# More filler matmuls and wider pick matmuls in an attention-decode and gMLP kernel

## Chip, cores, metric

One core of one Trainium2 chip. The metric is the device time of one execution in microseconds, lower is better. Before: 651.57 us, median of 6 runs (651.5 to 651.92). The span in the profile is about 1.4 us shorter than the measured time (650.2 against 651.6 us), because it runs from the first to the last recorded instruction.

## The reference

Branch A is attention for one query token with 32 heads over a cache of 16384 keys and values. Branch B is a small gated MLP on the same token. A sigmoid gate mixes them.

```python
q = (x @ wq) -> 32 heads of 128
scores = einsum('bhqd,bhkd->bhqk', q, k_cache) * 128 ** -0.5    # k_cache: 32 x 16384 x 128 bf16
p = softmax(scores); o = einsum('bhqk,bhkd->bhqd', p, v_cache)  # v_cache: the same size
a = o.reshape(1, 1, 4096) @ wo                                  # wo: 4096 x 512
b = gmlp(x)                                                     # a few MB of weights
return g * a + (1 - g) * b                                      # output: 1 x 1 x 512
```

K and V alone are 2 x 32 x 16384 x 128 x 2 bytes = 268 MB, and each byte is used once. With wq, wo and the MLP weights it is 279.6 MB.

## The kernel before

Heads are processed in 16 pairs. K and V of a pair are 8.4 MB each. The loads rotate through three buffers: K0, K1, V0, K2, V1, K3, ..., V14, V15 and then wo. A load waits until the buffer's last user has signalled. All the large loads are issued from one queue (SP).

For each pair VectorE (DVE) multiplies K by the query, TensorE (PE) sums parts of the products, DVE reduces, ScalarE (ACT) takes the exponential, and PE multiplies the weights with V. Four accumulators at array columns 0, 32, 64 and 96 collect the value sums. ACT copies them to SBUF, and four "pick" matmuls add the right rows into two columns of `o_ps` (the trace shows each of these fp32 matmuls as two, eight in all).

```python
    def warm(e, n):                 # n fillers of 128 columns, rhs all zeros
        for j in range(n):
            args = (m_ps[0], ident[:, :], zero[:, :])
            # ... the first loads weights, the others reuse them

    def fill(e, m, n=1):            # n fillers of m columns, at array column 96
        for _ in range(n):
            matmul_again(nc, e, m_ps[0][96:96 + m, :], ident[:, 0:m], zero[:, :], start=True,
                         stop=True, skip_group_check=True)

    def values(e, p, pa, va):
        # ... 8 groups: 8 value matmuls at columns 32 * (j % 4), one fill(e, 8)
        o2 = o_ps[:, bass.ds(value(e, p, NP - 1) * 2, 2)]
        fill(e, 8, 2)
        take(e, drn_s)                                  # ACT's copy of the accumulators
        for r in range(4):
            ins = e.matmul(o2, lhsT=d_sb[:, r * Dh:(r + 1) * Dh],
                           rhs=pick[:, r * 2:(r + 1) * 2], start=False, stop=False,
                           skip_group_check=True)
        ins.then_inc(pe.sem, 1)                         # frees the V buffer
```

Each filler streams 512 columns of zeros past m columns of the array (m is 128, 8 or 1; 379 ns each at the median, and two in a row start 0.215 us apart). The fillers write to a bank that nobody reads; their only use seems to be to keep PE busy, so that its clock stays up. The tail after the last pair normalizes o, transposes and gathers it with PE and DVE, and multiplies it by the 32 row blocks of wo. Sixteen blocks are done in four "wide" rounds, the other 16 in pairs of one-column matmuls at array columns 0 and 32. Those last rows wait for their part of wo.

```python
    def pe_wide(e):
        warm(e, 3)
        with e.Fori(0, WIDE // WG) as t:
            # ... 4 matmuls of one column, at columns 0, 32, 64, 96
            registers_first(nc, n, lambda: take(e, wo_s))
            ins.then_inc(pe.sem, 1)
            fill(e, 1)
            # ...
    # ACT copies d_ps to d_sb; then rows 16..31 of wo, each as two matmuls:
    for j, (a, b) in enumerate(zip(WO_CUTS[:-1], WO_CUTS[1:])):      # (0, 16, 24, 29, 31, 32)
        for k in range(max(a, WIDE), b):
            y_ok = add(o2[:, k:k + 1], wo[:, k * D:(k + 1) * D],
                       [(ld_o[j], 16)] if k == a else (), k == H - 1)
        if b == 24:
            add(ones_f[:, 0:1], d_sb[:, :], [w_ok])
```

The softmax here doesn't subtract the row's maximum and nothing guards it: scores larger than these inputs give would overflow.

Of the kernel before, what the change touches and what calls it, by code (L numbers as in the profile page):

```python
# [6 lines left out]
ALU = mybir.AluOpType  # L7
AX = mybir.AxisListType

FP32 = mybir.dt.float32  # L10
BF16 = mybir.dt.bfloat16

P = 128
Dh = 128
H = 32
NP = H // 2
# [16 lines left out]
NG = KP // 4  # L33
TG = 8
WG = 4
NT = NG // TG
ZB = F // 4
K_CUTS = (0, 128, 256)
# [45 lines left out]
def take(eng, sem, n=1):  # L84

    eng.wait_ge(sem, n).then_inc(sem, -n)  # L86
# [90 lines left out]
def gated_mix_kernel(nc, A_x, A_k_cache, A_v_cache, A_wq, A_wo, B_x, B_w_in, B_w_sp, B_b_sp,  # L177
                     B_w_out, gate_w, out):
    def sb(name, shape, dt):
        return nc.alloc_sbuf_tensor(name, shape, dt)  # L180
# [4 lines left out]
    p_t = sb("p_t", [P, 2 * NG * 8], BF16)  # L185
    s_sb = sb("s_sb", [P, KP], FP32)
    d_sb = sb("d_sb", [P, 512], FP32)
    zero = sb("zero", [P, 512], BF16)
# [6 lines left out]
    ident = sb("ident", [P, P], BF16)  # L195
    eps_t = sb("eps_t", [P, 1], FP32)
    sel = sb("sel", [H, 4 * (P + 1)], BF16)
    pick = sb("pick", [P, 4 * 2], FP32)
    wbf = sb("wbf", [P, 2], FP32)
    g_sb = sb("g_sb", [P, 1], FP32)  # L200
    gm_sb = sb("gm_sb", [P, 1], FP32)
# [9 lines left out]
    L_sb = sb("L_sb", [P, H], FP32)  # L211
# [3 lines left out]
    o2 = sb("o2", [P, H], BF16)  # L215
# [40 lines left out]
    pool, sp, pe, dve, act = (Queue(nc, e, n) for e, n in (  # L256
        (nc.gpsimd, "pool"), (nc.sync, "sp"), (nc.tensor, "pe"), (nc.vector, "dve"),
        (nc.scalar, "act")))
# [7 lines left out]
    def value(e, reg, top):  # L266
        return nc.snap(bass.RegisterHandles([reg]), min_val=0, max_val=top)
# [4 lines left out]
    ident_ok = pool.chain(lambda e: e.affine_select(  # L272
        out=ident[:, :], in_=ident[:, :], compare_op=ALU.not_equal, fill=1.0, base=0,
        pattern=[[-1, P]], channel_multiplier=1))
    for t in [sel, L_sb, p_t, zero]:
        p_zero = pool.op(lambda e, t=t: e.memset(t[:, :], 0.0), mark=True)
    sel_ok = (pool.sem, ident_ok[1] + 1)
    pool.raw(lambda e: e.nop().then_inc(exp_s, 1))


# [15 lines left out]
    for c in range(DC):  # L296
        x_ok = pe.op(lambda e, c=c: e.matmul(
            m_ps[1][:, c * P:(c + 1) * P], lhsT=x_row[0:1, c::DC], rhs=ones_row[0:1, :],
            start=True, stop=True), wait=[(ld_x, 16)] if c == 0 else (),
            mark=(c == DC - 1))  # L300
# [6 lines left out]
        out=sel[:, :].rearrange("h (i x) -> h i x", x=P + 1)[:, :, 0:P:4],  # L307
        in_=ident[0:H, 0:H].unsqueeze(1).broadcast_to([H, 4, H])), wait=[sel_ok],
        mark=True)
    dve.op(lambda e: e.tensor_reduce(  # L310
        out=pick[:, :].rearrange("p (r s) -> p s r", r=4),
        in_=ident[:, :].rearrange("p (g x) -> p x g", x=32)[:, 0:8, :]
        .rearrange("p (s r) g -> p s r g", r=4), axis=AX.X, op=ALU.add), wait=[ident_ok], mark=True)
    dve.op(lambda e: e.tensor_tensor(out=xg_row[:, :], in0=x_row[:, :], in1=gw_row[:, :],
                                     op=ALU.mult), wait=[(ld_g, 48)], mark=True)
    dve.op(lambda e: e.tensor_copy(out=xgw[:, 1:3], in_=wb_row[:, :]), mark=True)
    xgw_ok = dve.chain(lambda e: e.tensor_reduce(out=xgw[:, 0:1], in_=xg_row[:, :], axis=AX.X,  # L317
                                                 op=ALU.add))
# [3 lines left out]
                                    stop=True), wait=[xgw_ok], mark=True)  # L322
    act.op(lambda e: e.activation(out=g_sb[:, :], in_=g_ps[:, 0:1], func=ACT.Sigmoid),
           wait=[g_ok], mark=True)
# [54 lines left out]
    for h in range(2):  # L379
        zh = ps_all[:, 6 * h * 512:(6 * h + 2) * 512].rearrange("p (b x) -> p b x", b=2)[:, :, 0:ZB]  # L380
        dve.op(lambda e, h=h, zh=zh: e.tensor_tensor(  # L381
            out=zm[:, 2 * h * ZB:2 * (h + 1) * ZB].rearrange("p (b m k) -> p b m k", b=2, k=FhC),
# [5 lines left out]
        out=z[:, :].rearrange("p (e k) -> p e k", e=2),  # L388
        in_=zm.rearrange("p (e m k) -> p e k m", e=2, k=FhC), axis=AX.X, op=ALU.add))
    dve.chain(lambda e: e.scalar_tensor_tensor(  # L390
        out=zt[:, :], in0=z[:, :], scalar=0.044715, in1=z[:, :], op0=ALU.mult, op1=ALU.mult))
    zt_ok = dve.chain(lambda e: e.scalar_tensor_tensor(
        out=zt[:, :], in0=zt[:, :], scalar=1.0, in1=z[:, :], op0=ALU.add, op1=ALU.mult))
# [3 lines left out]
                  mark=True)  # L397
    dve.op(lambda e: e.tensor_tensor(out=z[:, :], in0=z[:, :], in1=zt[:, :], op=ALU.mult),
           wait=[sg_ok], mark=True)
    dve.chain(lambda e: e.tensor_reduce(out=stats[:, 0:1], in_=z[:, FhC:FC], axis=AX.X, op=ALU.add))  # L400
    dve.op(lambda e: e.tensor_tensor(out=sq[:, :], in0=z[:, FhC:FC], in1=z[:, FhC:FC],
                                     op=ALU.mult), mark=True)
    st_ok = dve.chain(lambda e: e.tensor_reduce(out=stats[:, 1:2], in_=sq[:, :], axis=AX.X,
                                                op=ALU.add))
    tot_ok = pe.op(lambda e: e.matmul(t_ps, lhsT=ones_f[:, :], rhs=stats[:, :],
                                      start=True, stop=True), wait=[st_ok], mark=True)
    dve.op(lambda e: e.tensor_scalar(out=mv[:, :], in0=t_ps, scalar1=1.0 / Fh,
                                     scalar2=0.0, op0=ALU.mult, op1=ALU.add), wait=[tot_ok],
           mark=True)
    var_ok = dve.chain(lambda e: e.scalar_tensor_tensor(  # L410
        out=var[:, :], in0=mv[:, 0:1], scalar=mv[:, 0:1], in1=mv[:, 1:2], op0=ALU.mult,
# [9 lines left out]
        out=u[:, :], in0=z2n[:, :], scalar=gm_sb[:, 0:1], in1=z[:, 0:FhC], op0=ALU.mult,  # L421
# [4 lines left out]
           mark=True)  # L426
# [3 lines left out]
        out=ps_all[:, 2 * 512:6 * 512].rearrange("p (n s x) -> p n s x", n=2, s=2)[:, :, 0, :],  # L430
# [32 lines left out]
    def v_buffer(e, reg, i):  # L463
        e.reg_alu(reg, i, 2, ALU.mult)
        e.reg_alu(reg, reg, 2, ALU.add)
        e.reg_alu(reg, reg, v_at[-1], ALU.min)
        e.reg_alu(reg, reg, 3, ALU.python_mod)


    def warm(e, n):  # L470
        for j in range(n):
            args = (m_ps[0], ident[:, :], zero[:, :])
            flags = dict(start=True, stop=True, skip_group_check=True)
            if j:
                matmul_again(nc, e, *args, **flags)
            else:
                e.matmul(args[0], lhsT=args[1], rhs=args[2], **flags)

    def fill(e, m, n=1):
# [3 lines that stand above are left out]
# [25 lines left out]
    def values(e, p, pa, va):  # L508
        v_buffer(e, va, p)
        e.reg_alu(va, va, 2 * ROW, ALU.mult)  # L510
        e.reg_alu(pa, p, 2, ALU.python_mod)
        e.reg_alu(pa, pa, 2 * NG * 8, ALU.mult)
        with e.Fori(0, NT) as t:
            p8 = p_t[:, bass.ds(t * (TG * 8), TG * 8)]
            v8 = bufs[:, bass.ds(t * (TG * 512), TG * 512)]
            n = len(nc.cur_bb.bb.instructions)
            for j in range(TG):
                ins = matmul_on(nc, e, lambda: matmul_at(
                    nc, e, d_ps, 32 * (j % 4), (8, 512), p8[:, 8 * j:8 * j + 8],
                    v8[:, j * 512:(j + 1) * 512], (p_t[:, 0:8], bufs[:, 0:512])),  # L520
                    [(va, 1024 * j), (pa, 16 * j)])
            registers_first(nc, n, lambda: take(e, v_s))
            ins.then_inc(pv_s, 1)
            fill(e, 8)
            e.reg_alu(va, va, 2 * TG * 512, ALU.add)
            e.reg_alu(pa, pa, 2 * TG * 8, ALU.add)
        o2 = o_ps[:, bass.ds(value(e, p, NP - 1) * 2, 2)]
        fill(e, 8, 2)
        take(e, drn_s)
        for r in range(4):  # L530
            ins = e.matmul(o2, lhsT=d_sb[:, r * Dh:(r + 1) * Dh],  # L531
                           rhs=pick[:, r * 2:(r + 1) * 2], start=False, stop=False,
                           skip_group_check=True)
        ins.then_inc(pe.sem, 1)

# [63 lines left out]
    def drain(e):  # L599
        take(e, pv_s, NT)  # L600
        return e.copy(out=d_sb[:, :], in_=d_ps)  # L601
# [38 lines left out]
    for n, kind, i in loads:  # L640
        wait = [user[n - 3]] if n >= 3 else [w_free] if buf[n % 3] is setup else []
# [4 lines left out]
        for a, b, done in zip(cuts[:-1], cuts[1:], sems):  # L646
            sp.op(lambda e, a=a, b=b, n=n, src=src: e.dma_start(
                out=buf[n % 3][:, a * Dh:b * Dh], in_=src[:, a * Dh:b * Dh]),
                wait=wait if a == 0 else (), inc=(done, 16))
    wo_src = A_wo.rearrange("(p k) n -> p (k n)", k=H)  # L650
    for j, (a, b) in enumerate(zip(WO_CUTS[:-1], WO_CUTS[1:])):
        sp.op(lambda e, a=a, b=b: e.dma_start(out=wo[:, a * D:b * D], in_=wo_src[:, a * D:b * D]),
              wait=[user[wo_at - 3]] if a == 0 else (), inc=(ld_o[j], 16))
# [5 lines left out]
    def pool_pairs(e):  # L659
        hand(e, ld_k[0], k_s, 2)  # L660
        with e.Fori(0, NP // 2 - 1):
            hand(e, ld_k[1], k_s, 2)
            hand(e, ld_v[0], v_s, NT)
            hand(e, ld_k[0], k_s, 2)
            hand(e, ld_v[1], v_s, NT)
        for j in range(len(ld_kh)):
            hand(e, ld_kh[j], k_s, 1)
        hand(e, ld_v[0], v_s, NT)
        for j, (a, b) in enumerate(zip(V_CUTS[:-1], V_CUTS[1:])):
            hand(e, ld_vp[j], v_s, (b - a) * NT // KP)  # L670

# [5 lines left out]
        out=o_sb[:, :], in0=o_ps[:, 0:H], scalar=g_sb[:, 0:1], in1=rl[:, :], op0=ALU.mult,  # L677
# [6 lines left out]
    for i in range(4):  # L684
        o2p_ok = pe.op(lambda e, i=i: e.matmul(
            l_ps[:, P:P + H], lhsT=sel[:, i * P:(i + 1) * P], rhs=oT[:, i * H:(i + 1) * H],
            start=(i == 0), stop=(i == 3)), wait=[oT_ok] if i == 0 else (), mark=(i == 3))
    o2_ok = dve.op(lambda e: e.tensor_copy(out=o2[:, :], in_=l_ps[:, P:P + H]), wait=[o2p_ok],
                   mark=True)

    def pool_wo(e):
        e.wait_ge(*d_zero)
        e.wait_ge(*o2_ok)
        for j, (a, b) in enumerate(zip(WO_CUTS[:-1], WO_CUTS[1:])):
            if a < WIDE:
                hand(e, ld_o[j], wo_s, (min(b, WIDE) - a) // WG)

    pool.raw(pool_wo)

    def pe_wide(e):  # L700
        va, pa = (counter(e, n, 0) for n in ("wa", "oa"))
        warm(e, 3)
        with e.Fori(0, WIDE // WG) as t:
            w8 = wo[:, bass.ds(t * (WG * D), WG * D)]
            o8 = o2[:, bass.ds(t * WG, WG)]
            n = len(nc.cur_bb.bb.instructions)
            for j in range(WG):
                ins = matmul_on(nc, e, lambda: matmul_at(
                    nc, e, d_ps, 32 * (j % 4), (1, D), o8[:, j:j + 1], w8[:, j * D:(j + 1) * D],
                    (o2[:, 0:1], wo[:, 0:D])), [(va, in_wo + 2 * j * D), (pa, 2 * j)])  # L710
            registers_first(nc, n, lambda: take(e, wo_s))
            ins.then_inc(pe.sem, 1)
            fill(e, 1)
            e.reg_alu(va, va, 2 * WG * D, ALU.add)
            e.reg_alu(pa, pa, 2 * WG, ALU.add)

# [19 lines left out]
    for q in (dve, act):  # L736
        mine = range(NC)[:NC // 2] if q is dve else range(NC)[NC // 2:]
        for s in mine:
            ok = q.op(lambda e, s=s, copy=(q is act): (e.copy if copy else e.tensor_copy)(  # L739
                out=res[0:1, s * DQ:(s + 1) * DQ], in_=a_ps[32 * s:32 * s + 1, 0:DQ]),  # L740
                wait=[y_ok] if s in mine[:1] else (), mark=(s == mine[-1]))
# [50 lines left out]
```

## Time and profile before

| | before |
|---|---|
| measured time | 651.57 us |
| span of the profiled run | 650.2 us |
| bytes loaded | 279.6 MB |
| rate from 2 to 640 us | 433 GB/s, DMA share 1.00 |
| PE busy, DVE busy | 65%, 52% |
| mean granted PE clock | 0.85 of full |

In all views PE stands for TensorE's matmuls, PEld for its weight loads, a trailing q (SPq, PEq) for an engine's instruction sequencer, and L106 for line 106 of the kernel. The granted clock is the share of full speed that TensorE was given.

These are lines of the profile page: busy time, share of the span and instruction count of each engine, and the load rate in 40 equal slices.

```profile
span 650.2 us, 7779 instructions
...
PE 423.5 (65%) x2474; PEld 47.0 (7%) x1312; DVE 335.2 (52%) x156; ACT 46.1 (7%) x114; POOL 2.6 (0%) x11
...
GB/s 384 463 419 452 452 387 452 452 444 395 452 452 395 444 452 444 395 452 452 407 431 452 444 395 452 452 427 411 452 452 391 448 452 439 399 431 472 390 431 342
```

PE is busy for 65% of the span and DVE for 52% (335.2 us), but the load stream is steady from the first slice on (384 to 472 GB/s, and 342 in the last slice). The next view gives whole stretches. Its columns are: stretch in us, busy time and count of each engine, granted clock, DMA share and GB/s.

```profile
core 0: us, PE busy (x) PEld busy (x) DVE busy (x) ACT busy (x) POOL busy (x), PEclk, DMA share, GB/s
2.00:640.00 638.00, 416.19 (x2400) 43.82 (x1244) 334.06 (x152) 44.58 (x112) 1.71 (x4) 0.85 1.00 433
640.00:648.50 8.50, 7.29 (x74) 3.21 (x68) 0.65 (x3) 1.06 (x2) 0.00 (x0) 1.00 0.85 345
```

For 638 us the DMA share is 1.00 at 433 GB/s, and the clock in the last 8.5 us is 1.00. That the loads can go no faster is my reading, from this share and from the runs below: over such a stretch the rate was 433 GB/s whether PE was busy 384 (no_fill), 416 or 515 us (gap40) of it.

The timeline shows how far ahead the load queue is and what ends the run. Columns: start, duration, engine, line, operation, operands, count, and in brackets the idle time before it and what ended it.

```profile
596.37 1.28 SPq L647 DMA_DIRECT2D bufs<-in_A_v_cache_dram  x3
...
631.08 1.03 PE L106 MATMUL ps_all<-bufs,p_t 128*8 x8 [2.06 <-PEq L86]
...
640.08 1.05 PE L531 MATMUL ps_all<-pick,d_sb 128*128 128x2 f32 x8 [0.37 <-PEq L86]
...
643.38 0.39 PE L106 MATMUL ps_all<-bufs,o 128*1 x4 [0.32 <-PEq L86]
...
645.91 0.38 PE L91 MATMUL ps_all<-zero,ident 128*1 128x512 bf16 x1
...
645.97 1.04 PE L724 MATMUL ps_all<-bufs,o 128*1 128x256 bf16 x16
...
647.28 0.42 PEld L724 LDWEIGHTS ps_all<-bufs,o 128*1 128x1 bf16 x10 [0.36 <-DMA bufs<-in_A_wo_dram]
...
647.96 0.09 PEld L724 LDWEIGHTS ps_all<-bufs,o 128*1 128x1 bf16 x4 [0.26 <-DMA bufs<-in_A_wo_dram]
648.23 0.08 PEld L724 LDWEIGHTS ps_all<-bufs,o 128*1 128x1 bf16 x2 [0.19 <-DMA bufs<-in_A_wo_dram]
...
648.58 0.41 DVE L739 CAST res<-ps_all 1x256 bf16<-1x256 f32 x1 [6.04 <-PE ps_all L724]
```

The picks of pair 13 end at about 596.3 us; the load of V15 (in three parts) goes into their buffer and is issued at 596.37. By the trace its first packets start only at about 617.7 us, behind the loads that are queued before it. So a pick that comes some microseconds later delays nothing here. At the end the rows of L724 wait three times for wo (0.36, 0.26 and 0.19 us), and the cast of the result follows the last row at once. So the end is tied to the landing of wo.

### The profile page before, as it was taken

The page shows a single profiled execution, that of the slowest core. Times are in us where ns is not written, and L with a number is a line of the kernel's source. Part 1 is how long each engine was busy: PE and PEld are TensorE (multiplying, and loading weights), DVE is VectorE, ACT ScalarE, POOL GpSimd, SP SyncE. Part 2 cuts the span into 40 slices and gives each one's busy share as a digit, 9 for nine tenths or more (in the row PEclk, how much of TensorE's full clock was granted, in tenths as well). Part 3 has the DMA queues.
Part 4 walks back from the last instruction along what each step waited for, and adds up shares of the span by engine and source line. Part 5 has one row for each costly group of instructions (what it writes and reads, how often), then busy time and mean ns, then how long its engine had stood idle before and what let it go on. Part 6 is the DMA issues. An engine that isn't in the chain of part 4 may idle for free. (4 is left out here: it accounts for less than half of the span.)

```text
span 650.2 us, 7779 instructions
## 1 busy us (share of the span) xinstructions
PE 423.5 (65%) x2474; PEld 47.0 (7%) x1312; DVE 335.2 (52%) x156; ACT 46.1 (7%) x114; POOL 2.6 (0%) x11
## 2 busy tenths in 40 slices
PE   0646687847477574857757486584748857478678
PEld 0000000000101000010000101000010100001022
DVE  3457839256280835618165370835628174465600
ACT  2220000100001000010100001000000100001011
POOL 1000000000000000000000000000000000000000
PEclk9959798958889796888969679796977969698979
DMA  9999989999999999999999999999999999999898
GB/s 384 463 419 452 452 387 452 452 444 395 452 452 395 444 452 444 395 452 452 407 431 452 444 395 452 452 427 411 452 452 391 448 452 439 399 431 472 390 431 342
DMA packets 6203, 279.60 MB, mean 430 GB/s; under 512 B 695, under 2 KB 826, under 8 KB 1210
## 3 DMA queue, kind: packets, MB, share of 16 engines
q1 hardware_dynamic: 6194, 279.58, 99.6%
q8 instruction: 1, 0.02, 0.0%
q10 hardware_dynamic: 8, 0.00, 0.0%
HBM read 279.58 MB, written 0.00 MB: 430 GB/s over the span
## 5 line engine op out<-in xcount | busy, mean ns | idle before, releaser
L579 DVE TENSOR_TENSOR bufs<-bufs,qb x64 | 281.4, 4418 | 171.8 <-DVEq L86 171.8
L91 PE MATMUL ps_all<-bufs,ident 128*128 x960 | 257.7, 422 | 0.0
L496 PE MATMUL ps_all<-bufs,ident 128*128 x64 | 28.8, 450 | 154.7 <-PEq L86 154.5
L106 PE MATMUL ps_all<-bufs,p_t 128*8 x1024 | 82.3, 395 | 30.3 <-PEq L86 20.3
L564 DVE TENSOR_REDUCE s_sb<-ps_all 128x64 f32<-128x512 f32 x64 | 44.0, 688 | 92.1 <-DVEq L86 92.1
L91 PE MATMUL ps_all<-zero,ident 128*8 128x512 bf16 (+2 forms) x167 | 59.4, 388 | 0.0
L592 ACT ACTIVATE p_t<-s_sb 64x256 f32 x32 | 13.3, 414 | 462.5 <-ACTq L86 462.1
L496 PEld LDWEIGHTS ps_all<-bufs,ident 128*128 128x128 bf16 x64 | 6.3, 99 | 365.3 <-issue 365.3
L106 PEld LDWEIGHTS ps_all<-bufs,p_t 128*8 x1024 | 19.3, 83 | 163.3 <-issue 161.9
L531 PE MATMUL ps_all<-pick,d_sb 128*128 128x2 f32 x128 | 17.3, 257 | 16.5 <-PEq L86 16.5
L531 PEld LDWEIGHTS ps_all<-pick,d_sb 128*128 128x128 f32 x128 | 16.0, 195 | 34.8 <-issue 34.8
L601 ACT COPY d_sb<-ps_all 128x512 f32<-128x512 f32 x16 | 9.4, 586 | 105.3 <-ACTq L86 105.3
L606 ACT CAST ps_all<-zero 128x512 f32<-128x512 bf16 x15 | 8.8, 589 | 1.7
L675 DVE RECIPROCAL rl<-ps_all 128x32 f32<-128x32 f32 x1 | 0.4, 358 | 12.3 <-PE ps_all L552 12.3
L381 DVE TENSOR_TENSOR bufs<-ps_all,ident 128x896 f32<-128x896 f32 x2 | 2.1, 1086 | 8.7 <-PE ps_all L91 8.7
L676 DVE SCALAR_TENSOR_TENSOR o_sb<-ps_all,g_sb,rl 128x32 bf16<-128x32 f32 x1 | 0.3, 251 | 11.7 <-PE ps_all L531 11.7
L592 ACT ACTIVATION_READ_ACCUMULATOR p_t<-s_sb x32 | 5.9, 185 | 0.0
L321 PE MATMUL ps_all<-xgw,const-float32-1.0 1*128 1x3 f32 x2 | 0.6, 359 | 8.0 <-DVE xgw L317 8.0
L91 PE MATMUL ps_all<-bufs,xb 128*128 x12 | 5.0, 547 | 0.0
L106 PE MATMUL ps_all<-bufs,u 128*1 x14 | 2.6, 372 | 3.1 <-ACT ps_all L427 2.4
L345 PE MATMUL ps_all<-bufs,xb 128*128 x4 | 2.3, 574 | 3.3 <-DMA bufs<-in_B_w_in_dram 3.3
L301 DVE MEMSET ps_all<- 128x3584 f32 x1 | 3.0, 3045 | 1.9 <-PEq L770 1.9
(76 smaller groups left out, 40.9 us busy)
## 6 DMA issues: line engine op xcount, KB each, us to landing
bufs<-in_A_k_cache_dram SPq DMA_DIRECT2D x2, 4096.0 KB, 36.3
bufs<-in_A_v_cache_dram SPq DMA_DIRECT2D x1, 5120.0 KB, 34.5
bufs<-in_A_wq_dram SPq DMA_DIRECT2D x1, 4096.0 KB, 12.4
bufs<-in_A_v_cache_dram SPq DMA_DIRECT2D x1, 2048.0 KB, 39.1
bufs<-in_A_wo_dram SPq DMA_DIRECT2D x1, 2048.0 KB, 25.5
bufs<-in_B_w_in_dram SPq DMA_DIRECT2D x1, 1792.0 KB, 15.6
bufs<-in_A_v_cache_dram SPq DMA_DIRECT2D x1, 1024.0 KB, 41.1
bufs<-in_A_wo_dram SPq DMA_DIRECT2D x1, 1024.0 KB, 27.7
```

The source lines that it names most:

```text
L91: ins = eng.matmul(out, lhsT=lhsT, rhs=rhs, **flags).ins
L106: ins = eng.matmul(bank[0:m, 0:n], lhsT=lhsT, rhs=rhs, **flags).ins
L301: dve.op(lambda e: e.memset(ps_all[:, 0:7 * 512], 0.0), mark=True)
L345: if n else matmul_on(nc, e, lambda: e.matmul(args[0], lhsT=args[1], rhs=args[2], **flags), [at, (xa, 0)]))
L381: dve.op(lambda e, h=h, zh=zh: e.tensor_tensor(out=zm[:, 2 * h * ZB:2 * (h + 1) * ZB].rearrange("p (b m k) -> p b m k", b=2, k=FhC), in0=z ...
L496: matmul_on(nc, e, lambda: e.matmul(s3, lhsT=ident[:, :], rhs=k3[:, :, 0:W], start=True, **flags), [(kw, 0)])
L531: ins = e.matmul(o2, lhsT=d_sb[:, r * Dh:(r + 1) * Dh], rhs=pick[:, r * 2:(r + 1) * 2], start=False, stop=False, skip_group_check=True)
L564: return e.tensor_reduce(out=s_sb[:, c * QK:(c + 1) * QK], in_=s_ps[c % 2].rearrange("p (j w) -> p j w", w=W), axis=AX.X, op=ALU.add)
L579: e.tensor_tensor(out=k3, in0=k3, in1=qi, op=ALU.mult).then_inc(mul_s, 1)
L592: e.activation(out=p_t[rows, bass.ds(at, NG * 8)].rearrange("p (t c) -> p t c", c=8)[:, :, 4 * s:4 * s + 4], in_=s_sb[rows, :].rearrange(" ...
L601: return e.copy(out=d_sb[:, :], in_=d_ps)
L606: e.copy(out=d_ps, in_=zero[:, :]).then_inc(drn_s, 1)
```

## The change

The intent, as the diff suggests it, is a warmer TensorE clock: a third filler before the picks of every pair, a fourth warm-up matmul before the wide rounds, two fillers instead of one in each round, and picks 64 columns wide (62 of them zeros), which keep the array busy longer than 2 columns do. The zeros are added to columns of `o_ps` that are added to later or not read. The whole diff:

```diff
--- before.py
+++ after.py
@@ -33,6 +33,7 @@
 NG = KP // 4
 TG = 8
 WG = 4
+PW = 64
 NT = NG // TG
 ZB = F // 4
 K_CUTS = (0, 128, 256)
@@ -195,7 +196,7 @@
     ident = sb("ident", [P, P], BF16)
     eps_t = sb("eps_t", [P, 1], FP32)
     sel = sb("sel", [H, 4 * (P + 1)], BF16)
-    pick = sb("pick", [P, 4 * 2], FP32)
+    pick = sb("pick", [P, 4 * PW], FP32)
     wbf = sb("wbf", [P, 2], FP32)
     g_sb = sb("g_sb", [P, 1], FP32)
     gm_sb = sb("gm_sb", [P, 1], FP32)
@@ -272,9 +273,9 @@
     ident_ok = pool.chain(lambda e: e.affine_select(
         out=ident[:, :], in_=ident[:, :], compare_op=ALU.not_equal, fill=1.0, base=0,
         pattern=[[-1, P]], channel_multiplier=1))
-    for t in [sel, L_sb, p_t, zero]:
+    for t in [pick, sel, L_sb, p_t, zero]:
         p_zero = pool.op(lambda e, t=t: e.memset(t[:, :], 0.0), mark=True)
-    sel_ok = (pool.sem, ident_ok[1] + 1)
+    sel_ok = (pool.sem, ident_ok[1] + 2)
     pool.raw(lambda e: e.nop().then_inc(exp_s, 1))
 
 
@@ -308,9 +309,9 @@
         in_=ident[0:H, 0:H].unsqueeze(1).broadcast_to([H, 4, H])), wait=[sel_ok],
         mark=True)
     dve.op(lambda e: e.tensor_reduce(
-        out=pick[:, :].rearrange("p (r s) -> p s r", r=4),
+        out=pick[:, :].rearrange("p (r x) -> p x r", r=4)[:, 0:2, :],
         in_=ident[:, :].rearrange("p (g x) -> p x g", x=32)[:, 0:8, :]
-        .rearrange("p (s r) g -> p s r g", r=4), axis=AX.X, op=ALU.add), wait=[ident_ok], mark=True)
+        .rearrange("p (s r) g -> p s r g", r=4), axis=AX.X, op=ALU.add), wait=[(pool.sem, ident_ok[1] + 1)], mark=True)
     dve.op(lambda e: e.tensor_tensor(out=xg_row[:, :], in0=x_row[:, :], in1=gw_row[:, :],
                                      op=ALU.mult), wait=[(ld_g, 48)], mark=True)
     dve.op(lambda e: e.tensor_copy(out=xgw[:, 1:3], in_=wb_row[:, :]), mark=True)
@@ -524,12 +525,12 @@
             fill(e, 8)
             e.reg_alu(va, va, 2 * TG * 512, ALU.add)
             e.reg_alu(pa, pa, 2 * TG * 8, ALU.add)
-        o2 = o_ps[:, bass.ds(value(e, p, NP - 1) * 2, 2)]
-        fill(e, 8, 2)
+        o2 = o_ps[:, bass.ds(value(e, p, NP - 1) * 2, PW)]
+        fill(e, 8, 3)
         take(e, drn_s)
         for r in range(4):
             ins = e.matmul(o2, lhsT=d_sb[:, r * Dh:(r + 1) * Dh],
-                           rhs=pick[:, r * 2:(r + 1) * 2], start=False, stop=False,
+                           rhs=pick[:, r * PW:(r + 1) * PW], start=False, stop=False,
                            skip_group_check=True)
         ins.then_inc(pe.sem, 1)
 
@@ -699,7 +700,7 @@
 
     def pe_wide(e):
         va, pa = (counter(e, n, 0) for n in ("wa", "oa"))
-        warm(e, 3)
+        warm(e, 4)
         with e.Fori(0, WIDE // WG) as t:
             w8 = wo[:, bass.ds(t * (WG * D), WG * D)]
             o8 = o2[:, bass.ds(t * WG, WG)]
@@ -710,7 +711,7 @@
                     (o2[:, 0:1], wo[:, 0:D])), [(va, in_wo + 2 * j * D), (pa, 2 * j)])
             registers_first(nc, n, lambda: take(e, wo_s))
             ins.then_inc(pe.sem, 1)
-            fill(e, 1)
+            fill(e, 1, 2)
             e.reg_alu(va, va, 2 * WG * D, ALU.add)
             e.reg_alu(pa, pa, 2 * WG, ALU.add)
 
```

## The prediction

> **What bounds the kernel now.** The load stream. The page gives 279.60 MB in a 650.2 us span. In a table of windows from 2 to 646 us the DMA share is 1.00 at 433 GB/s[...]. PE is busy 65%, DVE 52%. The last V load is released by pick matmuls (L531) at 596.3 us, issued at 596.4, and used only from 631 us (timeline; the DMA queue's own waits): the queue is some 20 us ahead. Until about 647 us TensorE time is worth nothing.
>
> Only the tail can matter. The timeline shows: last pick matmuls 640.08-641.1; o normalized 641.17; transpose and gather to 642.5; four rounds of wide matmuls at 643.38, 644.14, 644.89, 645.69; the L724 rows from 645.97. There the weight loads wait for DMA of wo three times (0.36, 0.26, 0.19 us idle, starting again at 647.28, 647.96, 648.23). The last matmul ends 648.55, then cast (0.41 us) and store. So the last rows of wo landing, plus about 2 us, set the end.
>
> **The change, costed.**
> 1. One more filler (fill 8, 3) before each pick: about 0.215 us at full clock (start to start of fillers). PE sits idle 1.08 us before most picks and 0.37 us before the last. Cost 0.
> 2. pick 64 columns instead of 2. A pick's eight weight loads start 0.111 us apart (189 ns each, overlapping) and set the pace. L724's fp32 matmuls of 256 columns start 0.216 us apart, so 64 columns are about 0.054 us (estimate), hidden under the next load except for the last: +0.05 us per pair, up to +0.4 if they don't overlap. It counts only after the last pair.
> 3. warm 4 instead of 3: fillers start at 642.24, .465, .68; a fourth would stream until about 643.11, before the wide matmuls at 643.38. Cost 0.
> 4. fill twice in a wide round: rounds are 0.755 us apart, paced by the sequencer; the matmuls and one filler stream 0.44 us, two 0.655 us. It fits; after the fourth round it puts L724 off by about 0.2 us. That meets the 0.36 us wait for DMA, so perhaps 0.05 us reaches the end.
> 5. A larger memset of pick (under 0.52 us of POOL, what zero takes) at the start; the first load that needs the set-up buffer is issued at 36.2 us behind queued K.
>
> **The intended gain** is a warmer TensorE. [...]granted clock 0.50 in 630.1-636.8, 1.00 in 636.9-648.6, mean 0.85. But the tail, where alone it could pay, is already at 1.00 and waits for wo. A warmer clock earlier only lengthens waits for DMA.
>
> **Predicted time:** 651.6 us, no change; 80% range 650.9 to 652.4 (before: 651.5 to 651.92). Faster by over 2%: 0.01; within 2%: 0.98; slower by over 2%: 0.01.
>
> **What would show it.** DMA share still 1.00 at 433 GB/s; L724's three waits for wo still there, the first shorter by about 0.2 us; last L724 matmul at 648.5-648.7; pick weight loads still 0.11 us apart; idle before picks down by 0.2 us; mean clock 0.85-0.95.
>
> **What would make it wrong.** If in many executions before the clock falls to 0.5 in the tail, fillers could save up to 1 us. If wide picks serialize with their weight loads, or fillers delay the rounds more than I read, the tail grows 0.3-0.5 us.

Two passages of it that no trace of this case shows are cut, where marked: a figure set beside the 433 GB/s, and a general statement about the clock. Neither is a term of the forecast's sum, which came to at most 0.1 us (0.05 for the last pick, perhaps 0.05 for the last round) on 651.57 us with no gain from the clock, and was put as 651.6.

## The result

After: 651.51 us, median of 6 runs (651.48 to 651.9); before 651.57 us. The ratio is 0.9999, with a 95% interval from 0.9986 to 1.0012. Ratios here are the mean time of one kernel's fast runs over that of the other's of the same rounds, without the first (profiled) run of each, so not quite the ratio of the medians quoted. The change makes no difference that can be measured.

The lines of the page after:

```profile
span 650.1 us, 7802 instructions
...
PE 434.9 (67%) x2496; PEld 46.5 (7%) x1312; DVE 335.6 (52%) x156; ACT 46.1 (7%) x114; POOL 2.9 (0%) x12
...
GB/s 387 468 411 452 452 395 444 452 440 399 452 452 403 436 452 444 395 452 452 419 419 452 452 391 448 452 427 411 452 452 391 448 452 440 399 436 468 390 430 343
```

PE is busy 11.4 us longer (434.9 - 423.5). The records show 22 more matmuls (2496 - 2474): the change adds 21 (16 before picks, 1 in the warm-up, 4 in the rounds), and one record is missing in the trace of before (L477 has three weight loads there but two matmuls; after, L478 has three of each). By the page's groups the fillers account for 4.8 us (64.2 against 59.4); most of the rest is the unchanged score matmuls, which took 265.2 instead of 257.7 us because more of them (224 against 183 of 1024, counted in the traces) fell into stretches at half clock, where one took 634 ns at the median instead of 379. Nothing in the load stream moved:

```profile
2.00:640.00 638.00, 426.59 (x2417) 43.34 (x1245) 334.44 (x152) 44.75 (x112) 1.96 (x5) 0.85 1.00 433
640.00:648.50 8.50, 8.35 (x80) 3.16 (x68) 0.67 (x4) 0.96 (x3) 0.00 (x0) 1.00 0.85 347
```

The load rate is still 433 GB/s at share 1.00, and the mean clock up to 640 us is still 0.85. In the last 8.5 us PE is busy 8.35 instead of 7.29 us, at a clock that was 1.00 already. The timeline of the tail after:

```profile
639.96 1.10 PE L532 MATMUL ps_all<-pick,d_sb 128*128 128x64 f32 x8 [0.16 <-PEq L87]
...
643.26 0.39 PE L107 MATMUL ps_all<-bufs,o 128*1 x4
...
645.79 0.38 PE L92 MATMUL ps_all<-zero,ident 128*1 128x512 bf16 x1
...
645.84 0.38 PE L725 MATMUL ps_all<-bufs,o 128*1 128x256 bf16 x4
...
646.01 0.38 PE L92 MATMUL ps_all<-zero,ident 128*1 128x512 bf16 x1
...
647.16 0.42 PEld L725 LDWEIGHTS ps_all<-bufs,o 128*1 128x1 bf16 x10 [0.35 <-DMA bufs<-in_A_wo_dram]
...
647.84 0.09 PEld L725 LDWEIGHTS ps_all<-bufs,o 128*1 128x1 bf16 x4 [0.26 <-DMA bufs<-in_A_wo_dram]
648.14 0.08 PEld L725 LDWEIGHTS ps_all<-bufs,o 128*1 128x1 bf16 x2 [0.21 <-DMA bufs<-in_A_wo_dram]
...
648.49 0.41 DVE L740 CAST res<-ps_all 1x256 bf16<-1x256 f32 x1 [6.04 <-PE ps_all L725]
```

Relative to the last picks the tail is the same as before within 0.1 us. The last rows still wait for wo three times, 0.35, 0.26 and 0.21 us. (All lines are one higher than before: L725 is L724.)

Two lines from the view of the tile `pick` for each kernel, first before, then after. They are the duration of the pick matmuls (minimum, median, maximum in ns) and the idle time of PE before them.

```profile
L531 PE MATMUL ps_all<-pick,d_sb x128: 251/251/354, 99.2 to 640.9; 128*128 128x2 f32 x128
...
  PEq L86: 16.5, 16
```

```profile
L532 PE MATMUL ps_all<-pick,d_sb x128: 275/275/318, 99.5 to 640.8; 128*128 128x64 f32 x128
...
  PEq L87: 13.1, 16
```

A wider pick matmul takes 24 ns longer at the median (275 - 251), and PE's idle time before picks falls by 3.4 us over 16 pairs, 0.21 us each, which is one filler. Both are visible, and neither reaches the end.

### The profile page after: what moved, and what is told of

It is laid out like the page before. It is cut to its first block, busy times and chain, and to the rows that moved or that the text cites. A ratio compares the mean times of both kernels' runs of the same rounds, so it can differ in the third digit from the quotient of the medians.

```text
span 650.1 us, 7802 instructions
## 1 busy us (share of the span) xinstructions
PE 434.9 (67%) x2496; PEld 46.5 (7%) x1312; DVE 335.6 (52%) x156; ACT 46.1 (7%) x114; POOL 2.9 (0%) x12
## 5 line engine op out<-in xcount | busy, mean ns | idle before, releaser
L92 PE MATMUL ps_all<-bufs,ident 128*128 x960 | 265.2, 432 | 0.0
L497 PE MATMUL ps_all<-bufs,ident 128*128 x64 | 28.5, 445 | 148.1 <-PEq L87 147.8
L92 PE MATMUL ps_all<-zero,ident 128*8 128x512 bf16 (+2 forms) x188 | 64.2, 388 | 0.0
L532 PE MATMUL ps_all<-pick,d_sb 128*128 128x64 f32 x128 | 17.6, 280 | 13.1 <-PEq L87 13.1
```

Source lines behind the costliest of these rows:

```text
L92: ins = eng.matmul(out, lhsT=lhsT, rhs=rhs, **flags).ins
L497: matmul_on(nc, e, lambda: e.matmul(s3, lhsT=ident[:, :], rhs=k3[:, :, 0:W], start=True, **flags), [(kw, 0)])
L532: ins = e.matmul(o2, lhsT=d_sb[:, r * Dh:(r + 1) * Dh], rhs=pick[:, r * PW:(r + 1) * PW], start=False, stop=False, skip_group_check=True)
```

## The experiments

The theory: the load stream sets the time up to the landing of wo; TensorE has slack, and the tail is already at full clock. Rivals: the parts of the change cancel each other; the clock does matter, but the change warmed too little; or the picks and the buffers that they free are on the critical path.

The profiled run of every experiment, and all of its timed runs, were fast. The kernel before was run beside each. One execution of the kernel before took 1306.57 us in the rounds of last6, last6_col0, gap40 and v_three_quarters; it counts as slow and is left out of the ratios. The median before in these four rows is that of its six fast runs. The record marks every run's result as correct, even those of the variants announced as wrong.

| run | median us | before, same rounds | ratio, 95% interval |
|---|---|---|---|
| fills_only | 651.59 | 651.65 | 0.9996 (0.9982 to 1.001) |
| picks_only | 651.70 | 651.65 | 1.0000 (0.9986 to 1.0013) |
| no_fill | 652.59 | 651.65 | 1.0015 (1.0001 to 1.0028) |
| flood | 653.83 | 651.65 | 1.0028 (1.0015 to 1.0042) |
| last6 | 651.56 | 651.77 | 0.9995 (0.9977 to 1.0013) |
| last6_col0 | 652.81 | 651.77 | 1.0017 (0.9999 to 1.0035) |
| gap40 | 664.29 | 651.77 | 1.0189 (1.0171 to 1.0207) |
| v_three_quarters | 589.56 | 651.77 | 0.9038 (0.9019 to 0.9056) |
| nw_before | 651.52 | 651.73 | 0.9996 (0.9982 to 1.001) |
| nw_after | 651.34 | 651.73 | 0.9999 (0.9985 to 1.0013) |
| flood5 | 651.57 | 651.80 | 0.9997 (0.9984 to 1.0011) |
| flood_late | 652.43 | 651.80 | 1.0009 (0.9995 to 1.0022) |

The timed runs alone resolve about 1 us; smaller statements below rest on the traces.

### fills_only and picks_only: do the parts cancel?

fills_only takes the three extra fillers, picks_only the wide picks.

```diff
-        fill(e, 8, 2)          # fills_only
+        fill(e, 8, 3)
-        warm(e, 3)
+        warm(e, 4)
-            fill(e, 1)
+            fill(e, 1, 2)
```

```diff
-    pick = sb("pick", [P, 4 * 2], FP32)     # picks_only, with all that belongs to it
+    pick = sb("pick", [P, 4 * PW], FP32)
```

> The three extra fillers of the change (3 instead of 2 before the picks, warm 4 instead of 3, two instead of one in a wide round), picks left 2 columns wide. Theory (the load stream sets the time, TensorE has slack until wo lands): within 0.15 us of the kernel before, 651.5 to 651.6. Rival (two parts of the change cancel, fillers gaining and wide picks costing): at least 0.3 us faster than before.

> Picks 64 columns wide, fillers as before. Theory: within 0.15 us of before; weight loads of a pick still 0.111 us apart; last pick's end about 0.05 us later after its start. Rival (parts cancel): at least 0.3 us slower than before.

Each is the same as before within its interval: medians -0.06 and +0.05 us. Neither interval excludes 0.3 us on timing alone (0.1% is 0.65 us), but the traces of both end like that of before, with three waits for wo (0.37, 0.24, 0.24 us and 0.36, 0.23, 0.23 us). That the parts cancel is not supported by anything seen.

### no_fill: what are the fillers worth at all?

```diff
     def warm(e, n):
+        return
     def fill(e, m, n=1):
+        return
```

> All fillers and warm-up matmuls removed from the kernel before. Theory: the granted clock falls (mean to about 0.6 to 0.7, 0.5 in the tail), yet nothing is lost up to about 640 us, DMA share stays 1.00 at 433 GB/s; the tail then runs at half clock and becomes bound by TensorE: 1 to 3 us slower, and L724's waits for wo shrink or vanish. Rival (the clock sets the time throughout): at least 15 us slower.

It is 0.94 us slower (medians), just under the expected 1 to 3 us. Two stretches of the run, and from its timeline the 16 rows of wo after the wide rounds and the cast:

```profile
2.00:640.00 638.00, 384.34 (x2237) 42.22 (x1240) 334.06 (x152) 44.42 (x111) 1.70 (x4) 0.84 1.00 433
640.00:648.50 8.50, 6.09 (x49) 3.07 (x51) 0.65 (x3) 1.18 (x2) 0.00 (x0) 0.60 0.86 349
```

```profile
646.20 1.91 PE L726 MATMUL ps_all<-bufs,o 128*1 128x256 bf16 x16
...
649.65 0.41 DVE L741 CAST res<-ps_all 1x256 bf16<-1x256 f32 x1 [6.95 <-PE ps_all L726]
```

Up to 640 us the clock hardly falls without fillers (0.84 against 0.85, with PE busy 384 instead of 416 us of the 638): the other matmuls were enough for that, and my guess of 0.6 to 0.7, which rested on no trace, was wrong. The load rate is the same 433 GB/s. The difference is in the tail: the clock there is 0.60 on average, because half speed was granted from 641.5 to 648.3 us (6.8 us; 0.50 in the window 641.6 to 648.2). The sixteen rows L726 take 1.91 us instead of 1.04, and the later rows no longer wait for wo. So the fillers that the kernel already had are worth about 1 us, all in the tail; with them the tail is at 1.00, and there was nothing left for more of them to gain.

### v_three_quarters: is it the load stream?

Wrong result.

```diff
         for a, b, done in zip(cuts[:-1], cuts[1:], sems):
+        # before this loop: if kind == "v" and 0 < i < NP - 1: cuts = (0, 3 * KP // 4)
```

> Wrong result on purpose: V loads of pairs 1 to 14 bring only three quarters of their columns, 14 x 2.10 MB = 29.4 MB less; all computing as before. Theory: faster by 29.4 MB / 433 GB/s = 67.8 us, so 583 to 585 us. Rival (TensorE or DVE sets the pace and the DMA is only as busy as they let it): less than 20 us faster.

It is 62.2 us faster with the same compute. The stretch from 2 to 560 us:

```profile
2.00:560.00 558.00, 406.35 (x2239) 37.61 (x1102) 333.40 (x151) 41.71 (x104) 1.69 (x4) 0.87 1.00 433
```

The rate is again 433 GB/s at share 1.00. In the trace the last packet of wo ends at 580.9 us (647.8 before), 66.9 us earlier, beside the estimated 67.8. The end moved by only 61.6 us (span 588.6 against 650.2). With the V loads shorter, the last pairs' compute lags behind the loads: the wide rounds start 1.3 us after the last packet of wo, no row waits for wo, and TensorE's own chain sets the tail. The theory holds for the stream; the expected time was missed because the end of this variant isn't the end of its loads.

### gap40: are the picks on the critical path?

```diff
-        fill(e, 8, 2)
+        fill(e, 8, 40)
```

> Forty instead of two fillers before each pick: 38 x 0.215 = 8.2 us more TensorE time in each of the 16 pairs (131 us in all), and V buffers freed that much later. Theory: pairs 1 to 14 cost nothing (DMA queue 20 us ahead); only the last two pairs' delay shows: 8 to 12 us slower than before, DMA share about 1.00 until 640 us. Rival (picks and the buffers they free are on the critical path): 60 to 130 us slower.

131 us of TensorE work was added, and the time rose by 12.5 us, a little above the expected range. Up to 640 us:

```profile
2.00:640.00 638.00, 515.08 (x2893) 38.99 (x1174) 333.76 (x151) 43.91 (x110) 1.69 (x4) 0.95 1.00 433
```

PE is busy 515 us of these 638 and the clock is 0.95, ten points higher than before; the load rate is unmoved at 433 GB/s. So much later buffer releases and a much warmer clock hardly touch the stream. They do a little: V1 is issued at 92.48 instead of 90.98 us, and from there to the end every load lands 0.7 us later than before (the last part of V15 at 638.97 against 638.27). It is the place where flood stalls (below). The rest of the 12.5 us is the delay of the last pairs, which piles up. In the profiled run, the slowest of the four (666.26 us), the last picks start at 655.26 us instead of 640.08, 15.2 us later, and the rows of wo then don't wait.

### flood, flood5, flood_late: would a warmer clock pay?

```diff
     def scores(...):               # after each quarter
+            for _ in range(10):    # flood5: 5; flood_late: 10, but none in the first two pairs
+                matmul_again(nc, e, m_ps[0], ident[:, :], zero[:, :], start=True, stop=True,
+                             skip_group_check=True)
             e.reg_alu(ka, ka, 2 * QK * Dh, ALU.add)
```

> Ten 128x512 fillers after each quarter of the score matmuls (2.15 us each at full clock, 64 times), otherwise as before. Theory: mean granted clock rises from 0.85 to 0.93 or more, PE busy rises by over 100 us, the time stays within 0.2 us of before because the load stream still sets it. Rival (a warmer clock is worth time and the change only warmed too little): over 1 us faster.

The clock rose to 0.906, but the run was 2.18 us slower. My expectation of no change failed, and the trace says where. Two stretches of before, then the same of flood, with the load rate in the last column:

```profile
90.00:105.00 15.00, 11.59 (x92) 2.15 (x73) 8.62 (x3) 2.19 (x6) 0.00 (x0) 0.89 1.03 446
105.00:120.00 15.00, 11.71 (x52) 0.29 (x3) 10.86 (x6) 0.00 (x0) 0.00 (x0) 1.00 1.07 463
```

```profile
90.00:105.00 15.00, 13.56 (x111) 2.51 (x73) 9.34 (x3) 2.19 (x6) 0.00 (x0) 1.00 1.00 415
105.00:120.00 15.00, 14.78 (x61) 0.29 (x3) 8.85 (x5) 0.00 (x0) 0.00 (x0) 0.89 0.98 424
```

From 75 to 90 us both load at 419 GB/s; flood then falls short by (446 - 415) x 15 + (463 - 424) x 15 GB/s times us = 1.05 MB, which is 2.4 us at 433 GB/s. Summing the packets of both traces gives 2.0 us late at 120 us, still 2.0 at 140, and 2.4 from 200 us to the end: most is lost in one place, and about 0.4 us more between 140 and 200 us. The issue of the second V load (V1) tells why the first loss happens. First before, then flood:

```profile
90.98 0.33 SPq L647 DMA_DIRECT2D bufs<-in_A_v_cache_dram  x1
```

```profile
95.64 0.33 SPq L650 DMA_DIRECT2D bufs<-in_A_v_cache_dram  x1
```

Fillers made the score quarters (5.6 us) slower than DVE's own pace (4.9 us), so V1's buffer came free at 95.64 us instead of 90.98. In the trace of flood no large packet is in flight from 95.57 us for 1.0 us; the trace of before has no such gap. There the queue is only some 4.6 us ahead, not the 20 us that I read at the end of the run.

> As flood, with 5 instead of 10 fillers after each quarter of the scores. In flood the score quarters took 5.6 us against DVE's 4.9 us, the second V load was issued at 95.64 us (90.98 before) and the load stream stood still once, from 95.57, for about 1 us plus ramp; it stayed some 2.3 us late to the end. Five fillers keep a quarter (3.6 + 1.1 us) below DVE's pace at full clock. Theory (flood lost its 2.2 us in that one stall): the second V load is issued before 93 us, no stall, within 0.2 us of before, clock above 0.87. Rival (fillers load something shared and slow the whole stream, or cost time in proportion): about 1.1 us slower.

> As flood with 10 fillers, but none in the first two pairs, the rest of the score matmuls unchanged. Theory (one stall at the start, because only there the queue is less than 5 us ahead): no stall, wo lands within 0.2 us of before, 0 to 0.5 us slower than before (the last values may start up to 0.5 us later). Rival (all 64 groups of fillers cost): about 14/16 of flood's 2.2 us, 1.9 us slower.

flood5 issues V1 at 91.95 us and has no gap; 651.57 us, no slower than before, at a clock of 0.869 (I had expected above 0.87). flood_late has no gap either, and its last load packets end at 647.72 us (647.76 before): so the stall, with the small loss after it, explains flood's late stream. But it is 0.63 us slower (span 651.1, 0.9 longer). From its timeline, the last picks and the cast:

```profile
641.49 1.05 PE L534 MATMUL ps_all<-pick,d_sb 128*128 128x2 f32 x8 [0.40 <-PEq L86]
...
649.49 0.41 DVE L746 CAST res<-ps_all 1x256 bf16<-1x256 f32 x1 [5.54 <-PE ps_all L731]
```

Its last picks start 1.4 us later than before's, and its last rows no longer wait for wo: here the tail is TensorE's, by more than the 0.5 us that I had allowed. Picks 1.4 us late moved the cast by only 0.9 us (649.49 against 648.58): TensorE's slack in the tail is about 0.5 us (gap40 gives the same: picks 15.2 us late, cast 14.7). The timed runs don't resolve the 0.63 us; the trace does. A mean clock of 0.898 gained nothing. Together: a warmer clock during the stream was worth nothing here, and fillers cost time where they delayed a buffer's release while the queue was shallow (flood, 2.18 us), or the last picks (flood_late, 0.9 us in its trace).

### nw_before and nw_after: what if wo were not the end?

Wrong result: rows 16 to 31 of wo are not loaded, rows 0 to 15 are used twice. Applied to both kernels.

```diff
+        if a >= WIDE: continue                    # no load of these rows
-            y_ok = add(o2[:, k:k + 1], wo[:, k * D:(k + 1) * D],
-                       [(ld_o[j], 16)] if k == a else (), k == H - 1)
+            y_ok = add(o2[:, k:k + 1], wo[:, (k - WIDE) * D:(k - WIDE + 1) * D], (), k == H - 1)
```

> Wrong result on purpose: the kernel before without loading rows 16 to 31 of wo (rows 0 to 15 are used twice), so no L724 row waits for DMA and DMA ends about 5 us earlier. Theory: TensorE's own chain is only about 0.25 us behind the landing of wo, so the end comes 0.1 to 0.4 us earlier than before (L724 then streams without a gap). Rival (the three waits of 0.36, 0.26, 0.19 us are all on the critical path): 0.8 us earlier.

> The same with the kernel after: the tail set by TensorE, so what fillers and wide picks cost there is no longer hidden by DMA. Theory: within 0.1 us of nw_before, since the last pick ends 0.05 us later and the fillers fit in gaps. Rival (they cost tail time which waiting for wo hid): 0.2 to 0.8 us slower than nw_before.

First nw_before, then nw_after: the rows of wo from the first one on, and the cast (for nw_after the first line holds the four rows that start before the second filler).

```profile
646.00 1.04 PE L726 MATMUL ps_all<-bufs,o 128*1 128x256 bf16 x16
...
648.41 0.41 DVE L741 CAST res<-ps_all 1x256 bf16<-1x256 f32 x1 [5.83 <-PE ps_all L726]
```

```profile
645.99 0.38 PE L727 MATMUL ps_all<-bufs,o 128*1 128x256 bf16 x4
...
648.40 0.41 DVE L742 CAST res<-ps_all 1x256 bf16<-1x256 f32 x1 [5.81 <-PE ps_all L727]
```

In nw_before the cast comes 2.41 us after the first row's start (648.41 - 646.00). In before it came 2.61 us after (648.58 - 645.97). So all three waits for wo together were worth only 0.20 us, although they add up to 0.81 us: between the waits the rows still have to stream through PE, and without waits that work takes most of the time anyway. The times agree (median 0.21 us less), but they don't resolve it.

With these three waits gone, nw_after's cast starts at 648.40 us against 648.41, from a first wide round at 643.40 against 643.42. So the doubled fillers of the rounds cost and gain 0.0 us within what a trace shows.

One wait for wo is left, though, before the first wide round, and I had overlooked it. In before the first part of wo is issued at 617.63 us and takes 25.5 us to land, so it lands at about 643.1. These are the issue from the timeline and the part's line on the page (KB, us to landing):

```profile
617.63 2.23 SPq L652 DMA_DIRECT2D bufs<-in_A_wo_dram  x5
...
bufs<-in_A_wo_dram SPq DMA_DIRECT2D x1, 2048.0 KB, 25.5
```

The round starts at 643.38, 0.2 us after that landing, and so it does in after and both nw runs. It comes 3.29 to 3.30 us after the start of the last picks in all four. Where the picks are so late that wo is there already (gap40, flood, flood_late, v_three_quarters) it comes 2.91 to 2.92 us after them. So about 0.4 us of work between the last picks and the first round is hidden in all four runs, and what the wider last pick (0.05 us) and the fourth warm-up would cost without this wait is not shown.

### last6 and last6_col0: do fillers hold up the rows behind them?

After the last wide round comes a filler that precedes the first rows in program order. I had predicted that a second one puts the rows off by 0.2 us; the trace of after shows them starting at 645.84, ahead of the second filler at 646.01. So six fillers more, once at array column 96 as in the kernel, once at column 0, which the rows use.

```diff
             e.reg_alu(pa, pa, 2 * WG, ALU.add)
+        fill(e, 1, 6)          # last6
+        # last6_col0: the same six with output m_ps[0][0:1, :]
```

> Six more fillers of one column at array columns 96 to 127 after the last wide round, before the L724 rows, which use columns 0 and 32. In-order rival (a matmul starts only when the earlier ones have started, as the prediction's step 4 assumed): the first L724 matmul comes about 1.3 us (6 x 0.215) later than before, the end 0.8 to 1.1 us later. Theory from the trace of after (L725 starts ahead of the second filler): the first L724 matmul is still about 0.05 us after the first filler's start, end unchanged within 0.15 us.

> The same six fillers at array column 0, which the first row of every L724 pair uses. Both accounts: L724's rows at column 0 wait for the fillers, so they start about 1.3 us later; the 0.36 us wait for wo and about 0.1 us of the later ones absorb part; the end comes 0.7 to 1.1 us later.

last6 (L725 is the rows, L91 the fillers):

```profile
645.86 0.38 PE L91 MATMUL ps_all<-zero,ident 128*1 128x512 bf16 x1
...
645.93 0.38 PE L725 MATMUL ps_all<-bufs,o 128*1 128x256 bf16 x4
...
646.08 0.38 PE L91 MATMUL ps_all<-zero,ident 128*1 128x512 bf16 x1
...
647.23 0.42 PEld L725 LDWEIGHTS ps_all<-bufs,o 128*1 128x1 bf16 x10 [0.34 <-DMA bufs<-in_A_wo_dram]
...
648.56 0.41 DVE L740 CAST res<-ps_all 1x256 bf16<-1x256 f32 x1 [6.04 <-PE ps_all L725]
```

The first rows start 0.07 us after the first filler; the six others, all earlier in the program, start among the rows, one each 0.215 us until 647.16. The end is where it was (span 650.2). With column 0, three rows at column 32 start between the fillers (646.17, 646.60, 647.03), and the rows at column 0 only after all of them, at 647.24; the end is 1.1 us later in the trace (span 651.3). That the three are those at column 32 is read from their order in the program; the trace names no columns. So in these two runs matmuls at other array columns passed queued ones (rows at 645.93, fillers from 646.08), and those at the same column waited (647.24). How far ahead they may pass these runs don't tell, nor do they show that one increment on the last matmul issued covers earlier ones at other columns.

## Why the prediction was right

- **Bound by loads: right.** 433 GB/s in before and after, and in no_fill, gap40 and flood5, at mean clocks from 0.84 to 0.95; 29.4 MB less made the loads 66.9 us shorter.
- **"Until about 647 us TensorE time is worth nothing": too strong.** The tail follows TensorE's chain closely. In before the last eight value matmuls start at 638.46 us, 0.2 us after the last part of V15 lands (638.27), the first wide round 0.2 us after the first part of wo lands, and the three later waits are worth 0.20 us. Work added there has about 0.5 us of room: flood_late used it up and paid 0.9 us in its trace. The change stayed within it, so the forecast of its time did not suffer.
- **Extra filler before picks: right.** Cost 0; idle before picks fell by 0.21 us each.
- **Picks 64 columns wide: right.** From the start of the last picks to the next DVE instruction it took 1.14 us after (639.96 to 641.10) and 1.09 before (640.08 to 641.17): +0.05 us, as estimated. The matmuls overlap their weight loads (after: loads from 639.95 to 640.92, matmuls from 639.96 to 641.06); the rival of +0.4 us did not occur.
- **Fourth warm-up: right.** The first wide round came 3.30 us after the start of the last picks in both (643.26 - 639.96, 643.38 - 640.08). The prediction saw that the warm-up fits in the gap; what makes the gap, the wait for the first part of wo, it did not name.
- **Two fillers per round: the rounds right, the step after them wrong.** Rounds stayed 0.75 to 0.80 us apart. "After the fourth round it puts L724 off by about 0.2 us" failed: the rows started on time (645.84, ahead of the second filler at 646.01; they use other array columns, and in last6 they passed six more), and the first wait for wo was 0.35 us, not 0.16. The sum did not suffer, since I had let only 0.05 us of it reach the end: here a wrong step happened to cost nothing.
- **"The queue is some 20 us ahead": right at the end, too general.** At V1 it is 4.6 us ahead (flood). The change adds 0.2 us per pair there, so it did not matter.
- **No gain from the clock: right.** The tail's clock was 1.00 in the profiles of before and after; in those of fills_only, picks_only, nw_before and nw_after the tail's fillers (0.38 us) and rounds (0.39 us, against 0.59 to 0.60 in no_fill) take as long as in before. Without any fillers the tail loses about 1 us (no_fill: 0.94 in the medians, the cast 1.07 us later); my "up to 1 us" for a tail at half clock was the right size, and the case did not arise in the profiles. Whether it arises in executions that were not profiled stays open; their times leave room for a few tenths of a microsecond.

No run that does all the work was faster than before by more than its interval, so no better version is offered. What is left outside the stream is 1.0 us before the first large packet and 2.4 us from the last one (647.76) to the end.

## What to carry to other kernels

Before warming a clock, find out which stretch waits for TensorE; here, with the DMA share at 1.00 and the rate at 431 to 433 GB/s whatever the clock (0.84 to 0.95), only the work tied to the last loads could gain, and the clock had to be read there (1.00), not as the mean of the run (0.85). A queue's lead has to be read at each point of the run: the same fillers that left the stream in time where more was in hand (flood_late, last packet at 647.72 us against 647.76) stalled it for 1.0 us where 4.6 us were left (flood). Waits that add up to 0.8 us in a profile were worth 0.2 us here (nw_before), since the engine had queued work that filled most of the time between them.
